# Three more warming matmuls at the start of a fused attention and MLP kernel, tied to the first chunk's statistics

## The chip, the cores and the metric

The kernel runs on one core of a Trainium2 chip. The metric is the device time of one execution in microseconds (us). The profiled span, from the first to the last instruction, is about 1.8 us shorter than the time (697.2 us against 695.4 in the profiled run of before).

## The reference, cut to what matters

```python
xn = layernorm(x)                      # x: 2048 tokens x 1024
out = x + attention(xn, wq, wk, wv, wo, beta) + mlp(layernorm(xn), w1, b1, w2, b2)
# mlp mixes tokens: u = gelu(h^T @ w1 + b1)   (contracts over the 2048 tokens)
```

The first product that TensorE can do is `h^T @ w1`, where h is the normalized input. It contracts over tokens, so it can begin as soon as the first chunk of 128 tokens is normalized, and it continues chunk by chunk (16 chunks).

## The kernel before: the parts that matter

The kernel has a small helper that follows every buffer as a resource with a last writer and a list of readers. A new operation waits for the last writer of what it reads, and for the last writer and all readers of what it writes:

```python
for r in reads:
    add(r.w)
    ...
for r in writes:
    ...
    for t in r.r.values():     # every recorded reader since the last write
        add(t)
```

At the start, while the input is being loaded, TensorE multiplies a zeroed tile ten times. Nobody reads the result:

```python
with fw.group(reads=[self.R_warm], writes=[self.R_bank[0]]):
    for _ in range(self.N_WARM):           # N_WARM = 10
        fw.mm(self.bank(0), self.warm[:, 0:P], self.warm[:], start=True, stop=True)
```

The norm of the chunks is written as a string of words, which gives the order of the operations on each engine:

```python
NORM_ORDER = (["D0 A1 S0 d2 h0 A1' A3 S1 d2' h1"] + ...)
# D0: statistics of chunk 0 on VectorE (two bn_stats, one bn_aggr); d2, d2': the two halves for chunk 2
# A1, A1': statistics of chunk 1 on ScalarE (odd chunks are done there)
# S0: rstd(0): a tensor_scalar on VectorE, then a power on GpSimd
# h0: scale_h(0): h = (x - mean) * rstd, on VectorE; TensorE's first real matmul waits for it

def rstd(self, c):
    ...
    fw.op("dve", lambda e: e.tensor_scalar(var, ..., E_H, op0=ALU.mult, op1=ALU.add), reads=[R], writes=[R])
    #                                       R is self.R_st[c], the statistics of chunk c
    fw.op("pool", lambda e: e.tensor_tensor(rs, var, self.expo[:, 0:1], op=ALU.pow), reads=[R, ...], ...)
```

`rstd` **writes** `R_st[c]`: it adds the epsilon to the variance in place.

The softmax here doesn't subtract the row's maximum and nothing guards it: scores larger than these inputs give would overflow.

## Time and profile before

| | before |
|---|---|
| time, median of the first 3 runs | 697.68 us (697.3, 697.68, 699.26) |
| span of the profiled run | 695.4 us |
| TensorE busy | 685.7 us, 99% |
| warming matmuls | 1.25 to 5.70 us, starts 0.427 us apart |
| granted clock turns full (record in the trace) | 5.84 us |
| first real matmul | 7.09 us, the next ones 0.216 us apart |

The granted clock is the profile's record of TensorE's clock, as a share of its full one. In this trace, equal matmuls start 0.427 us apart before it turns full at 5.84 us and 0.216 us apart after. Warming matmuls are there to be busy early, so that it turns full before real work; what that is worth is measured in run 7, where with four of them the real matmuls are 0.427 us apart until 10.5 us.

The page's busy times. Each entry is an engine's busy time, its share of the span and its number of instructions.

```profile
## 1 busy us (share of the span) xinstructions
PE 685.7 (99%) x4746; PEld 326.5 (47%) x4830; DVE 257.2 (37%) x581; ACT 277.7 (40%) x333; POOL 100.4 (14%) x156
```

The waits of TensorE (PE) over the whole span: who was waited for, us in total, how many times, the longest.

```profile
PE ps_all L194 <- DVE h L656: 1.4, 1, 1.4
PE ps_all L194 <- DVE brow L517: 1.3, 1, 1.3
PE ps_all L194 <- issue: 0.3, 2, 0.2
```

PE never waits for another engine for long after its first real matmul. So the kernel is bound by PE from then on, and whatever moves that first matmul moves the end.

The timeline of the start. Columns: start in us, duration in us, engine, line, operation, output and inputs with their shapes; in brackets how long the engine had been idle before, and who ended that. VectorE is DVE and GpSimd is POOL.

```profile
1.25 4.45 PE L194 MATMUL ps_all<-warm 128*128 128x512 bf16 x10 [1.25 <-DVE brow L517]
5.05 0.21 DVE L620 BATCH_NORM_AGGREGATE ln_mv<-ln_st 128x2 f32<-128x12 f32 x1
5.29 0.15 DVE L639 TENSOR_SCALAR ln_mv<-ln_mv 128x1 f32<-128x1 f32 x1
5.53 0.55 POOL L641 TENSOR_TENSOR ln_rs<-ln_mv,expo 128x1 f32<-128x1 f32 x1 [3.96 <-DVE ln_mv L639]
5.94 0.69 DVE L617 BATCH_NORM_STATS2 ln_st<-xin 128x6 f32<-128x512 bf16 x1 [0.49 <-DMA xin<-in_A_x_dram]
6.55 0.72 DVE L656 TENSOR_SCALAR h<-xin,ln_mv,ln_rs 128x512 bf16<-128x512 bf16 x2
7.09 1.46 PE L194 MATMUL ps_all<-h,w1early 128*128 128x512 bf16 x6 [1.39 <-DVE h L656]
```

This is the chain S0 (L639), power (L641), d2 (L617, which waited for the load of chunk 2), h0 (L656), first real matmul. PE is idle for 1.39 us between warming and work. DVE takes its instructions in order. Here h0 stands behind d2 and starts at 6.55 us, as d2 is ending.

### The profile page before, as it was taken

Reading aid. Unit: us, or ns where it says so; the run is one execution under the profiler, and the core shown is the slowest. Engines: PE = TensorE matmul, PEld = TensorE weight load, DVE = VectorE, ACT = ScalarE, POOL = GpSimd, SP = SyncE. Lnnn points to the kernel's source line nnn. Section 1 sums busy time; section 2 is a strip of 40 time slices with the busy share of each in tenths; the row PEclk is TensorE's granted clock in tenths of the full one; section 3 lists DMA queues with packets and bytes.
Section 4 is the critical chain, followed back from the end, with each engine's and each line's share of the span. In section 5 each row is a group of like instructions: output and inputs, shape, how many; then the busy total and the mean of one; then the engine's idle time right before and its main releaser. Section 6 shows DMA issues by size and latency. Waiting matters only on the chain.

```text
span 695.4 us, 11228 instructions
## 1 busy us (share of the span) xinstructions
PE 685.7 (99%) x4746; PEld 326.5 (47%) x4830; DVE 257.2 (37%) x581; ACT 277.7 (40%) x333; POOL 100.4 (14%) x156
## 2 busy tenths in 40 slices
PE   8999999999999999999999999999999999999998
PEld 3444444444444444444444445444444444445454
DVE  7740000000011334333436455536445553434445
ACT  7521211111134444444455444454544444534440
POOL 2600000000001111111121211112121111121130
PEclk9999999999999999999999999999999999999999
DMA  9497684227036536645263544525273544437014
GB/s 315 110 218 175 151 224 123 77 60 140 1 133 121 109 67 131 115 109 126 47 129 95 117 95 90 129 47 137 64 150 80 97 95 73 97 64 152 9 31 137
DMA packets 210537, 77.17 MB, mean 111 GB/s; under 512 B 173112, under 2 KB 202808, under 8 KB 210488
## 3 DMA queue, kind: packets, MB, share of 16 engines
q1 hardware_dynamic: 210344, 76.42, 47.8%
q8 instruction: 38, 0.62, 0.4%
q14 instruction: 11, 0.09, 0.1%
q10 hardware_dynamic: 144, 0.03, 0.0%
HBM read 59.79 MB, written 5.24 MB: 94 GB/s over the span
## 4 chain that ended last, share of the span: by engine, by line
PE 97%; DMA 1%; issue 1%; SPq 1%; DVE 0%
PE ps_all L194 97%; DMA xin<-in_A_x_dram 1%; SPq L216 1%; DVE ln_st L617 0%; DVE fin L1051 0%; PE ps_all L200 0%
## 5 line engine op out<-in xcount | busy, mean ns | idle before, releaser
L194 PE MATMUL ps_all<-gT,w2h 128*128 128x512 bf16 x868 | 207.8, 380 | 1.6 <-issue 0.2
L811 ACT ACTIVATE pT<-ps_all 128x512 bf16<-128x512 f32 (+1 forms) x128 | 151.4, 1234 | 76.7 <-PE ps_all L194 76.7
L194 PE MATMUL ps_all<-h,w1s 128*128 128x512 bf16 x752 | 165.1, 379 | 0.8
L806 POOL TENSOR_SCALAR_AFFINE_SELECT pT<-pT 128x512 bf16<-128x512 bf16 x128 | 83.9, 680 | 557.5 <-ACT pT L811 557.5
L194 PEld LDWEIGHTS ps_all<-gT,w2h 128*128 128x128 bf16 x896 | 83.1, 98 | 105.7 <-issue 13.8
L194 PEld LDWEIGHTS ps_all<-h,w1s 128*128 128x128 bf16 x768 | 75.1, 98 | 90.6
L845 DVE CAST ost<-ps_all 128x264 bf16<-128x264 f32 (+1 forms) x128 | 49.2, 398 | 169.4 <-PE ps_all L194 169.3
L713 ACT ACTIVATE gT<-ps_all,b1c 128x512 bf16<-128x512 f32 x56 | 35.1, 687 | 142.0 <-PE ps_all L194 136.4
L755 DVE CAST kT<-ps_all 128x512 bf16<-128x512 f32 x32 | 22.0, 688 | 176.9 <-PE ps_all L194 176.9
L194 PE MATMUL ps_all<-xnT,wk 128*128 128x512 bf16 x256 | 60.5, 379 | 0.0
L194 PE MATMUL ps_all<-xnT,wq 128*128 128x512 bf16 x256 | 60.4, 378 | 0.0
L194 PEld LDWEIGHTS ps_all<-vA,pT 128*128 128x128 bf16 x1280 | 47.7, 96 | 22.6
L194 PE MATMUL ps_all<-wv_sb,xnT 128*128 128x512 bf16 x227 | 54.0, 379 | 1.6
L739 ACT ACTIVATE qT<-ps_all 128x512 bf16<-128x512 f32 x32 | 19.1, 597 | 77.8 <-PE ps_all L194 77.8
L194 PE MATMUL ps_all<-vA,pT 128*128 128x33 bf16 x1280 | 48.6, 178 | 0.0
L951 DVE SCALAR_TENSOR_TENSOR stg<-ps_all,b2c,stg 128x512 bf16<-128x512 f32 x32 | 24.0, 750 | 61.7 <-PE ps_all L194 61.6
L758 ACT ACTIVATE etmp<-kT 128x512 bf16<-128x512 bf16 x24 | 15.1, 629 | 59.0 <-DVE kT L755 59.0
L194 PEld LDWEIGHTS ps_all<-xnT,wk 128*128 128x128 bf16 x256 | 23.8, 98 | 23.1
L194 PEld LDWEIGHTS ps_all<-wv_sb,xnT 128*128 128x128 bf16 x256 | 23.5, 97 | 23.7
L194 PEld LDWEIGHTS ps_all<-xnT,wq 128*128 128x128 bf16 x256 | 23.4, 97 | 23.2
L773 ACT ACTIVATE vA<-ps_all 128x512 bf16<-128x512 f32 x32 | 19.2, 600 | 37.1 <-PE ps_all L194 37.1
L194 PE MATMUL ps_all<-qT,kT 32*128 32x384 bf16 (+3 forms) x512 | 31.9, 299 | 0.0
(70 smaller groups left out, 419.7 us busy)
## 6 DMA issues: line engine op xcount, KB each, us to landing
w2h<-in_B_w_dram SPq DMA_DIRECT2D x32, 448.0 KB, 4.8
w1s<-in_B_w_dram SPq DMA_DIRECT2D x12, 1024.0 KB, 5.8
wq<-in_A_wq_dram SPq DMA_DIRECT2D x32, 256.0 KB, 4.4
wk<-in_A_wk_dram SPq DMA_DIRECT2D x32, 256.0 KB, 5.1
stg<-in_A_x_dram SPq DMA_DIRECT2D x16, 256.0 KB, 3.0
out_dram<-stg SPq DMA_DIRECT2D x16, 256.0 KB, 2.0
xin<-in_A_x_dram SPq DMA_DIRECT2D x2, 1024.0 KB, 10.5
wv_sb<-in_A_wv_dram SPq DMA_DIRECT2D x2, 1024.0 KB, 9.0
```

The costliest lines, as they stand in the source:

```text
L194: ins = self.nc.tensor.matmul(*args, **kwargs)
L216: ins = es.eng.dma_start(out_ap, in_ap, transpose=True) if transpose else es.eng.dma_start(out_ap, in_ap)
L713: fw.op("act", lambda e: e.activation(self.gT[:, fc, half * 512:(half + 1) * 512], self.bank(b), ACT.Gelu_apprx_tanh, bias=self.b1c[:, fc: ...
L739: fw.op("act", lambda e: e.activation(self.qT[k][:], self.bank(b), ACT.Copy), reads=[self.R_bank[b]], writes=[self.R_qT[k]])
L755: fw.op("dve", lambda e: e.tensor_copy(self.kT[k][:], self.bank(b)), reads=[self.R_bank[b]], writes=[self.R_kT[k]])
L758: fw.op("act", lambda e: e.activation(self.etmp[1][:], self.kT[k][:], ACT.Exp), reads=[self.R_kT[k]], writes=[self.R_etmp[1]])
L773: fw.op("act", lambda e: e.activation(self.vA[i][:, c, :, 0:D_HEAD], self.bank(b).rearrange("p (h d) -> p h d", d=D_HEAD), ACT.Copy), read ...
L806: fw.op("pool", lambda e: e.affine_select(d, d, pattern=[[0, 4], [1, P]], compare_op=ALU.is_ge, fill=0.0, base=0, channel_multiplier=-1), ...
L811: self.fw.op("act", lambda e: e.activation(dst, src, ACT.Exp, scale=SCALE), reads=R_src, writes=R_dst)
L845: fw.op("dve", lambda e: e.tensor_copy(dst, self.ps[:, b, 0:n * VW]), reads=[self.R_bank[b]], writes=[self.R_ost[o][qb]])
L951: fw.op("dve", lambda e: e.scalar_tensor_tensor(dst, self.bank(b), self.b2c[:, c:c + 1], dst, op0=ALU.add, op1=ALU.add), reads=[self.R_ban ...
```

## The change

Its intent is to keep TensorE active in that gap, so that its clock is full when real work begins. Three more warming matmuls are issued, and they are made to wait for the first chunk's statistics so that they come late enough.

```diff
-        with fw.group(reads=[self.R_warm], writes=[self.R_bank[0]]):
-            for _ in range(self.N_WARM):
+        self.keep_warm(self.N_WARM)
+
+    def keep_warm(self, n, reads=()):
+        fw = self.fw
+        with fw.group(reads=[self.R_warm, *reads], writes=[self.R_bank[0]]):
+            for _ in range(n):
                 fw.mm(self.bank(0), self.warm[:, 0:P], self.warm[:], start=True, stop=True)
...
-    NORM_ORDER = (["D0 A1 S0 d2 h0 A1' A3 S1 d2' h1"] +
+    NORM_ORDER = (["D0 W0 A1 S0 d2 h0 A1' A3 S1 d2' h1"] +
...
+            elif kind == "W":
+                self.keep_warm(3, [self.R_st[c]])
```

## The prediction

The forecast's sum came to 698.4 us: the times of before, plus the delay of the first real matmul (0.65 to 1.4 us), less what unlucky runs win back. Without that term, the two lower times of before (697.3 and 697.68) plus the 0.9 us as in the profile give 698.2 to 698.6 us. An unlucky phase is a start in which the clock turns full only after real work has begun; that there are such starts was a guess when this was written, and run 1 shows one.

> **What bounds the kernel now.** TensorE. The page gives PE 685.7 of 695.4 us (99%), and the chain of waits is 97% matmuls. PE's waits are only at the start: 1.3 us for the first memset, then 1.4 us before the first real matmul (`h,w1early`). So what moves the first real matmul (7.09 us) moves the end alike. From that one on they start every 0.216 us: the clock is full.
>
> **The start of before, from the timeline.** Ten warming matmuls start at 1.25 us, 0.427 us apart (slow clock); the last ends at 5.70. The trace's record of the granted clock turns full at 5.84 us. PE is idle from 5.70 to 7.09. DVE meanwhile: statistics of chunk 0 end at 5.26, the small tensor_scalar on its variance (L639) 5.29 to 5.44, POOL's power 5.53 to 6.08, statistics of chunk 2 from 5.94 (waited for its load), first half of h0 from 6.55, PE at 7.09.
>
> [...] full clock 4.6 us after PE's start. In an unlucky phase, before would get it only after real work began[...]. The times 697.3, 697.68 and 699.26 would fit two lucky runs and an unlucky one: a guess.
>
> **What the change does.** Its three matmuls wait for chunk 0's aggregation (5.26 us), which is earlier than the tenth warming matmul lets go (5.49), so that wait is free. They fill 5.49 to about 6.5 us (clock granted as in the profile) or to 6.98 us (all slow: 2 × 0.427 + 0.634 after 5.49).
>
> **The hidden cost.** The new group is recorded as a reader of chunk 0's statistics, R_st[0]. The next writer of that resource is the L639 tensor_scalar of chunk 0. It must now wait until the warming matmuls are done, which protects nothing. DVE is in order, so chunk 2's statistics, h0, S1 and h1 all move too. From the same steps of chunk 1 in the trace, tensor_scalar start to h start is 0.91 us; h0 start to PE's first matmul is 0.54 us. So PE starts at T + 1.45, T being the end of the warming plus about 0.05: about 8.0 us (+0.9) as in the profile, 8.5 us (+1.4) if all slow, 7.75 (+0.65) in the luckiest phase. The gap is moved rather than filled. After that DVE needs 1.33 us a chunk and PE 1.73: nothing more is lost or regained.
>
> **Gain.** The warming activity lasts to 6.5–7.0 us, so more phases get full clock before real work[...]. Fewer outliers, slower fast runs.
>
> **Prediction:** 698.4 us, 8 in 10 between 697.5 and 699.4. Faster by over 2%: 0.005; within 2%: 0.99; slower: 0.005.
>
> **What would show it.** Right: 13 warming matmuls; DVE's first L639 at about 6.6–7.1 us, waiting for PE, instead of 5.29; first real matmul at 7.75–8.5 us; all later work shifted equally; a smaller spread of times. Wrong: L639 still at 5.3 us and PE at 7.1; or PE stalling later, so that the delay is absorbed.
>
> **What would make it wrong.** [...]

## The result, and the profile after

The ratios are the mean time of one kernel's fast runs over that of the other's of the same rounds, so they are not quite the ratio of the medians.

| | before | after |
|---|---|---|
| median of 6 runs each | 697.53 us (697.14 to 699.26) | 697.95 us (697.7 to 698.36) |
| ratio | | 1.0001, 95% interval 0.9988 to 1.0014 |
| span of the profiled run | 695.4 us | 696.5 us |
| first real matmul | 7.09 us | 8.20 us |
| from the first real matmul's start to the last matmul's start | 685.798 us | 685.794 us |

The last line is worked out from the start times in the two traces. All work after the start takes the same time to 4 ns, so the start alone explains the difference of the two profiled runs: 1.11 us later at the first real matmul, 1.1 us more at the end.

The same lines of the timeline, after (S0 is now L645, the power L647, d2 L623, h0 L662):

```profile
1.25 5.38 PE L194 MATMUL ps_all<-warm 128*128 128x512 bf16 x13 [1.25 <-DVE brow L517]
4.93 0.21 DVE L626 BATCH_NORM_AGGREGATE ln_mv<-ln_st 128x2 f32<-128x12 f32 x1
6.74 0.15 DVE L645 TENSOR_SCALAR ln_mv<-ln_mv 128x1 f32<-128x1 f32 x1 [1.60 <-PE ps_all L194]
6.81 0.68 DVE L623 BATCH_NORM_STATS2 ln_st<-xin 128x6 f32<-128x512 bf16 x1
6.98 0.55 POOL L647 TENSOR_TENSOR ln_rs<-ln_mv,expo 128x1 f32<-128x1 f32 x1 [5.41 <-DVE ln_mv L645]
7.64 0.73 DVE L662 TENSOR_SCALAR h<-xin,ln_mv,ln_rs 128x512 bf16<-128x512 bf16 x2
8.20 0.38 PE L194 MATMUL ps_all<-h,w1early 128*128 128x512 bf16 x1 [1.57 <-DVE h L662]
```

The third line is the important one. S0, a 0.15 us operation on one value per row, had its input ready at about 5.1 us and stood idle for 1.60 us, released by PE. PE's warming ended at 6.63 us. The waits of DVE in the first 10 us show this wait as new, and the wait of 0.49 us for chunk 2's load gone, since d2 now comes after a later S0. Before, there were two waits for loads, chunk 0's (2.3 us) and chunk 2's:

```profile
DVE ln_st L617 <- DMA xin<-in_A_x_dram: 2.8, 2, 2.3
```

After, only chunk 0's is left, and S0's wait for PE has come:

```profile
DVE ln_st L623 <- DMA xin<-in_A_x_dram: 2.2, 1, 2.2
DVE ln_mv L645 <- PE ps_all L194: 1.6, 1, 1.6
```

The gap before the first real matmul is 1.57 us, where it had been 1.39. The added matmuls did not fill it; they pushed it.

Why, then, is the ratio 1.0001 and not 1.0016? The times of before are not all alike, and the experiments had to say how.

### The profile page after: what moved, and what is told of

Same layout as the page of the kernel before. It is cut to its first block, busy times and chain, and to the rows that moved or that the text cites. A ratio compares the mean times of both kernels' runs of the same rounds, so it can differ in the third digit from the quotient of the medians.

```text
span 696.5 us, 11235 instructions
## 1 busy us (share of the span) xinstructions
PE 686.7 (99%) x4749; PEld 326.8 (47%) x4833; DVE 257.2 (37%) x581; ACT 277.6 (40%) x333; POOL 100.1 (14%) x156
## 4 chain that ended last, share of the span: by engine, by line
PE 99%; issue 1%; DVE 0%; POOL 0%; DVEq 0%
PE ps_all L194 99%; POOL ln_rs L647 0%; DVE h L662 0%; DVE fin L1057 0%; DVE warm L515 0%; PE ps_all L200 0%; DVE ln_mv L645 0%; DVE brow L517 0%; DVEq L69 0%
```

## The experiments

The main theory has two parts. (1) The three matmuls are recorded as readers of `R_st[0]`, and S0 writes it, so S0 waits for them (a write-after-read wait), and everything behind it on DVE waits too. (2) What the change gains is in executions in which the clock turned full only after real work had begun. The rivals: the three matmuls delay the work simply by occupying PE or by waiting for the statistics; and the spread of before is noise that has nothing to do with the start.

The runs came in three calls. Kernels of one call share a chip and the runs of the kernel before, and each call was on another chip.

### 1. Before, unchanged

> The kernel before, unchanged, as a null control and for another look at the clock. Theory (two kinds of execution: the clock is granted either before or after the first real matmul at about 7.1 us): times fall in two groups, about 697.2 and about 698.5 to 699.3, and the profile shows the granted clock either before 7.1 us with every real matmul 0.216 us apart, or later, with the first real matmuls 0.427 us apart. Rival (the spread is noise from elsewhere): the start looks the same in every profile whatever the time. Ratio to before 1.000 within 0.001.

Measured: 698.2 us median of 6 runs, ratio 1.0004 (0.9991 to 1.0017). This profile was taken on an execution of the slower kind, 698.52 us, span 696.8. The stretch from 7.10 to 9.80 us of both executions of the same kernel, first the one of the beginning (columns: stretch, its length, busy time and number of matmuls in it, granted clock, DMA share, GB/s):

```profile
7.10:9.80 2.70, 2.70 (x13) 1.00 1.04 379
```

and this one:

```profile
7.10:9.80 2.70, 2.70 (x7) 1.00 1.01 358
```

PE is fully busy in both, but does 13 matmuls in one and 7 in the other. Here the real matmuls start 0.427 us apart, and 0.216 us apart only from about 10 us on. From the first real to the last matmul this execution took 687.27 us, 1.47 us more than the other. Its start is otherwise the same (first real matmul at 6.95 us). Beware of the column of the granted clock: it says 1.00 in both. In this trace there is no record of the clock's change at all, and where there is one, the stretches before it are shown as 1.00 too (5.00 to 5.80 us in the first profile, with the record at 5.84). The spacing of equal matmuls is the better witness.

All 41 runs of before fall into two groups with nothing between 697.88 and 698.52: 24 runs with a mean of 697.33 us, and 17 with a mean of 698.81. The difference, 1.48 us, is the 1.47 us of the trace. So the two starts differ as the theory says, which the rival of noise from elsewhere does not explain. That all 17 are slow-clock starts is inferred from this match and from one trace of each kind; if so, they are not rare: 17 of 41.

### 2. After, unchanged

> The changed kernel, unchanged, in the same rounds as the variants. Theory (write-after-read wait moves the start of the work by 0.65 to 1.4 us, and the clock is always granted in time): times 697.7 to 698.4, no run below 697.6 and none above 698.8; L645 waits about 1.5 us for PE; first real matmul at 7.75 to 8.5 us. Rival (the three matmuls are free and the difference is noise): times from 697.2 on.

Measured: 697.8 to 698.62 us, ratio 1.0008 (0.9996 to 1.002). S0 at 6.29 us after waiting 1.0 us for PE; first real matmul at 7.746 us. In this execution the clock turned full at 4.70 us by its record, so the warming ended sooner, at 6.17 us; the prediction had given 7.75 us for this case. That it fits so exactly is partly luck: the warming ended 0.08 us earlier than the 6.25 us behind that figure, and the way from there to the work was 0.08 us longer. The wait for PE was shorter than the "about 1.5 us" that I wrote, for that reason. Over both calls, after has 11 runs, from 697.7 to 698.62, with a mean of 698.13. It has one group only, between the two of before: 0.81 us above its fast group, 0.68 us below its slow one. No trace shows an execution of after with a slow-clock start.

### 3. The same matmuls without the dependence

```diff
-    N_WARM = 10
+    N_WARM = 13
```

(on the kernel before)

> Thirteen warming matmuls in one group, none of which reads the statistics: the same PE work as the change, without its dependence. Theory (the write-after-read wait is the cost): the small tensor_scalar of chunk 0 is back at about 5.3 us, the first real matmul at about 7.1 us, clock granted by about 7 us; times 697.1 to 697.6 in nearly every run, about 0.7 to 0.9 us below the changed kernel, and a smaller spread than before. Rival (three more matmuls occupy PE and that is the delay): first real matmul at about 8 us and times as the changed kernel, about 698.

Measured: 697.89 us median, five runs 696.86, 696.98, 697.89, 697.89, 697.91; ratio 0.9996 (0.9984 to 1.0008). None of the five lies in my range of 697.1 to 697.6. S0 was back at 5.17 us, as the theory says, though PE did all 13 matmuls. But the first real matmul was at 7.81 us, which no theory had expected. The timeline says why:

```profile
5.17 0.15 DVE L639 TENSOR_SCALAR ln_mv<-ln_mv 128x1 f32<-128x1 f32 x1
5.41 0.55 POOL L641 TENSOR_TENSOR ln_rs<-ln_mv,expo 128x1 f32<-128x1 f32 x1 [3.84 <-DVE ln_mv L639]
6.66 0.69 DVE L617 BATCH_NORM_STATS2 ln_st<-xin 128x6 f32<-128x512 bf16 x1 [1.33 <-DMA xin<-in_A_x_dram]
7.27 0.72 DVE L656 TENSOR_SCALAR h<-xin,ln_mv,ln_rs 128x512 bf16<-128x512 bf16 x2
7.81 0.81 PE L194 MATMUL ps_all<-h,w1early 128*128 128x512 bf16 x3 [1.01 <-DVE h L656]
```

The power for chunk 0 was done at 5.96 us, but h0 stands behind d2 on DVE, and d2 waited until 6.66 us for the load of chunk 2, which had come at 5.94 us in the first profile of before. It may be a second, smaller source of spread: the two groups of this kernel's times, 0.9 us apart, would fit it, but only one of the five was traced. The run doesn't decide against occupancy by its time, only by S0. The next three do.

### 4. The same change, one word moved

```diff
-    NORM_ORDER = (["D0 W0 A1 S0 d2 h0 A1' A3 S1 d2' h1"] +
+    NORM_ORDER = (["D0 A1 S0 W0 d2 h0 A1' A3 S1 d2' h1"] +
```

The three matmuls still wait for the statistics, in fact for S0 itself. But S0 is the last writer of `R_st[0]`, so nobody waits for them.

> The change with its word W0 moved behind S0: the three matmuls still wait for the first chunk's statistics (now for the tensor_scalar at about 5.4 us), but no writer of that resource comes after them. Theory (write-after-read): as the thirteen without a wait, first real matmul at about 7.1 us, 697.1 to 697.6. Rival (waiting for the statistics itself, or PE occupancy, is the cost): as the changed kernel, about 698, first real matmul at about 8 us.

Measured: 697.1 us median (696.93 to 697.67), ratio 0.9993 (0.9981 to 1.0005).

```profile
1.25 5.22 PE L194 MATMUL ps_all<-warm 128*128 128x512 bf16 x13 [1.25 <-DVE brow L517]
5.17 0.15 DVE L645 TENSOR_SCALAR ln_mv<-ln_mv 128x1 f32<-128x1 f32 x1
5.85 0.69 DVE L623 BATCH_NORM_STATS2 ln_st<-xin 128x6 f32<-128x512 bf16 x1 [0.52 <-DMA xin<-in_A_x_dram]
6.46 0.72 DVE L662 TENSOR_SCALAR h<-xin,ln_mv,ln_rs 128x512 bf16<-128x512 bf16 x2
7.00 1.67 PE L194 MATMUL ps_all<-h,w1early 128*128 128x512 bf16 x7 [0.53 <-DVE h L662]
```

Thirteen warming matmuls, a wait for the statistics, and the first real matmul at 7.00 us. The gap is now 0.53 us. Neither occupancy nor the wait on the statistics is the cost.

The same kernel was run once more later on:

> The change with W0 behind S0 once more, for more samples in the same rounds. Theory: no run above 698.1; median 697.1 to 697.5, about 0.8 us below the changed kernel's eleven runs so far (mean 698.15) and below the mean of before by about 0.6.

Measured: 697.13 us median (696.76 to 697.44), ratio 0.9989 (0.9977 to 1.0002), first real matmul at 6.86 us. (The mean of the changed kernel's eleven runs is 698.13, not the 698.15 of this expectation.)

### 5. The wait kept in its place, the record of the reader taken away

```diff
-        with fw.group(reads=[self.R_warm, *reads], writes=[self.R_bank[0]]):
+        with fw.group(reads=[self.R_warm], writes=[self.R_bank[0]], extra=[r.w for r in reads]):
```

The matmuls use none of the statistics, so nothing can race.

> The change with its order kept, but the three matmuls wait for the aggregation's token without being recorded as readers of the statistics (they use none of that data, so nothing races). Theory (write-after-read): the small tensor_scalar of chunk 0 back at about 5.3 us, first real matmul at about 7.1 us, times 697.1 to 697.6. Rival (the wait of PE for the statistics costs): as the changed kernel, about 698.

Measured: 697.26 us median (697.17 to 697.71), ratio 0.999 (0.9977 to 1.0003). S0 at 5.12 us, first real matmul at 7.27 us (d2 waited for its load until 6.11 us here):

```profile
5.12 0.15 DVE L645 TENSOR_SCALAR ln_mv<-ln_mv 128x1 f32<-128x1 f32 x1
6.11 0.69 DVE L623 BATCH_NORM_STATS2 ln_st<-xin 128x6 f32<-128x512 bf16 x1 [0.84 <-DMA xin<-in_A_x_dram]
7.27 2.10 PE L194 MATMUL ps_all<-h,w1early 128*128 128x512 bf16 x9 [0.91 <-DVE h L662]
```

The write-after-read part of the theory holds with the order of the words untouched.

### 6. One and six recorded readers

```diff
-                self.keep_warm(3, [self.R_st[c]])
+                self.keep_warm(1, [self.R_st[c]])      # and 6 in the other kernel
```

> One recorded reader instead of three. Theory (write-after-read, DVE waits for the end of the last recorded warming matmul): it ends at about 6.1 us, the small tensor_scalar starts at about 6.15, the first real matmul at about 7.6 us, 0.5 us later than before and 0.5 us earlier than with three. Rival (occupancy of PE): about 7.1 us, since PE is free by 6.1.

> Six recorded readers instead of three. Theory (write-after-read): the warming ends about 0.65 us later than with three if the clock is full by then (3 x 0.216), up to 1.28 us later if slow; the small tensor_scalar and the first real matmul move by the same amount, to 8.7 to 9.5 us; times 698.4 to 699.5. Rival (occupancy): PE is free at about 7.2 to 8.2 us, so the first real matmul would be at no more than about 8.2.

Measured for one: 697.84 us median of 4 (697.4 to 699.04), ratio 1.0 (0.9984 to 1.0017); S0 at 6.25 us, first real matmul at 7.70. Measured for six: 698.4 us median of 4 (698.33 to 698.83), ratio 1.0007 (0.9992 to 1.0022); S0 at 6.78, first real matmul at 8.24. The position for six missed my range of 8.7 to 9.5 us, because I had started from the run whose clock turned full at about 6.1 us (by the spacing of its matmuls), and in this one it was at 4.78. What the write-after-read theory says without knowing the clock is that the first real matmul follows the end of the warming at a fixed distance. It does:

| kernel (profiled run) | end of the warming | first real matmul | difference |
|---|---|---|---|
| three readers, first profile | 6.628 us | 8.200 us | 1.572 |
| three readers, second profile | 6.167 | 7.746 | 1.579 |
| one reader | 6.129 | 7.701 | 1.572 |
| six readers | 6.657 | 8.235 | 1.578 |
| ten matmuls, three of them readers (run 8) | 6.090 | 7.663 | 1.573 |
| nothing for S0 to wait for: before, twice | 5.701, 5.700 | 7.090, 6.946 | 1.389, 1.246 |
| nothing for S0 to wait for: runs 3, 4 (twice), 5 | 6.807, 6.475, 6.264, 6.361 | 7.814, 7.000, 6.857, 7.269 | 1.007, 0.525, 0.593, 0.908 |

The ends of the warming are the profile's, which models the ends of matmuls; that S0 starts 0.11 to 0.12 us after that end in all five runs with readers is as much as these traces say of it.

### 7. Four warming matmuls

```diff
-    N_WARM = 10
+    N_WARM = 4
```

(on the kernel before)

> The kernel before with four warming matmuls instead of ten, so that warming ends at about 3.2 us. Theory (too little early activity leaves the clock slow when real work starts): the first real matmul is still at about 7.1 us, but the matmuls after it are 0.427 us apart for a few us until the clock is granted [...]; times 1.5 to 3 us above the fast runs of before, 698.7 to 700.2. If times stay at 697.2, the warming matmuls have no worth and the spread of before has another cause.

Measured: 698.94 us median of 4 (698.84 to 700.55), ratio 1.0021 (1.0001 to 1.0041); the run at 700.55 lies above my range of 698.7 to 700.2. The first real matmul was at 6.72 us, earlier than in the two profiles of before, since chunk 2's load was early (d2 started at 5.33 us, right behind S0). But the matmuls were 0.427 us apart until 10.5 us, and the clock's record turns full at 10.87. From the first to the last real matmul it took 687.83 us, 2.03 us more than with a full clock. So warming has a worth, and part (2) of the theory holds from this side too.

### 8. The dependence without more work

```diff
-    N_WARM = 10
+    N_WARM = 7
```

(on the changed kernel: ten warming matmuls as before, the last three of them recorded readers)

> The dependence without extra work: ten warming matmuls as before, but the last three are the recorded readers of the statistics. Theory (write-after-read): they start at about 5.15 us, when the statistics are there, end at about 6.2 to 6.7, and the first real matmul is at the end of the warming plus 1.57 us as in the four runs with a reader so far, 7.8 to 8.3 us, though PE does no more work than before. Rival (the number of matmuls is the cost): first real matmul at about 7.1 us.

Measured: the first real matmul at 7.66 us, S0 at 6.21 after waiting 0.99 us for PE, 1.573 us from the end of the warming to the work:

```profile
1.25 3.17 PE L194 MATMUL ps_all<-warm 128*128 128x512 bf16 x7 [1.25 <-DVE brow L517]
5.27 0.82 PE L194 MATMUL ps_all<-warm 128*128 128x512 bf16 x3 [0.85 <-DVE ln_mv L626]
6.21 0.15 DVE L645 TENSOR_SCALAR ln_mv<-ln_mv 128x1 f32<-128x1 f32 x1 [0.99 <-PE ps_all L194]
7.66 0.81 PE L194 MATMUL ps_all<-h,w1early 128*128 128x512 bf16 x3 [1.57 <-DVE h L662]
```

The first real matmul is a little below my range of 7.8 to 8.3, since the clock turned full at 5.16 us and the three ran fast. The matmul count is that of before, and the delay is there: it is the dependence. The times are 697.76, 700.22, 700.28 and 700.68 us, ratio 1.0027 (1.0008 to 1.0046). The profile fell on the first of these. I had given no time for it. The three at 700 would fit a late start with a late clock on top, and the warming is interrupted here from 4.42 to 5.27 us. But no trace shows one of them, and no run shows what such a gap does to the clock, so this stays open.

### 9. h0 ahead of d2

```diff
-    NORM_ORDER = (["D0 W0 A1 S0 d2 h0 A1' A3 S1 d2' h1"] +
+    NORM_ORDER = (["D0 A1 S0 W0 h0 d2 A1' A3 S1 d2' h1"] +
```

> The change with W0 behind S0, and h0 moved ahead of d2 as well. In the runs so far, h0 stands behind d2 on DVE, and d2 waits for the load of chunk 2, which landed between 5.3 and 6.7 us; in the thirteen without a wait it landed at 6.66 us and the first real matmul was at 7.81. Theory (the second spread of the times, 696.9 against 697.9, is this landing): with h0 first, the first real matmul is at about 6.7 us in any case, bounded by the statistics of chunk 0, and no run is above 697.7. Since h1 then comes a little later, PE may wait for it at chunk 1, so the fastest runs could be up to 0.2 us slower than with d2 first. Rival (the second spread is not from this landing): same two groups of times, 696.9 and 697.9.

Measured: 697.19 us median (697.14 to 697.52), ratio 0.9992 (0.9978 to 1.0006). First real matmul at 6.71 us, as expected. But PE then waited in the first 12 us:

```profile
PE ps_all L194 <- DVE brow L517: 1.3, 1, 1.3
PE ps_all L194 <- DVE ln_mv L645: 0.6, 1, 0.6
PE ps_all L194 <- DMA w1early<-in_B_w_dram: 0.4, 1, 0.4
PE ps_all L194 <- DVE h L662: 0.2, 1, 0.2
```

The third line is the wait before the first real matmul:

```profile
6.71 1.89 PE L194 MATMUL ps_all<-h,w1early 128*128 128x512 bf16 x8 [0.43 <-DMA w1early<-in_B_w_dram]
```

The profile puts it down to a load of weights, but the matmul starts 0.56 us after h0 (6.15 us), as in the other runs (0.54 to 0.56), so that load held it up by next to nothing. The last line, 0.2 us for h, is new and lies inside the work. It is at chunk 1: from 8.21 to 8.79 us two matmuls start 0.58 us apart instead of 0.216. The work as a whole took 0.39 us longer (686.18 us from the first to the last real matmul), 0.36 of it there. So the earlier start (0.29 us against run 4) was given back at chunk 1. The spread of the five runs is 0.4 us, the smallest here, and there is no second group; the median is that of run 4. That agrees with the landing of chunk 2 as the second source of spread, but five runs are few for it.

## Why the prediction was right, and where it was off

The time, 697.95 us, lay in the range of 697.5 to 699.4 around 698.4, and the sum was made of the right terms. The time alone is a weak test, since the median of before, 697.53, lies in that range too; the starts in the trace are the stronger one.

- **What bounds it.** Right. From the first real matmul on, the work takes 685.79 to 685.92 us in 10 of the 13 profiles. The other three are the two with a slow clock in the work and the one with h0 first.
- **The hidden wait.** Right in kind and place. S0 waited for PE, 1.60 us, and it goes away with the reader's record (run 5), with the order (run 4), and comes without any additional matmul (run 8). Its reach was a little undersized: from the end of the warming to the first real matmul I took 1.50 us, and it measured 1.57. With warming that ended at 6.63 us instead of 6.5, this is why the first real matmul came at 8.20 us and not at the forecast 8.0.
- **The wait on the statistics being free.** Right: the eleventh matmul started at 5.495 us, 0.427 after the tenth, as if there were no wait. (In run 2, where the clock turned full at 4.70 us, PE seems to have waited a little: the warming ended 0.88 us after the statistics, 6.17 against 5.29 us, as in run 8, 6.09 against 5.21, where the profile shows that wait.)
- **The gain in unlucky phases.** Right in kind: 1.47 to 1.48 us were measured. The share of such phases was a guess from three runs, one in three. It is 17 of 41. That is the term that moved the ratio: against the fast group the change costs 0.81 us, against the slow one it wins 0.68. The mean over all runs is 697.94 us before and 698.13 after, and the ratio of six runs each happened to be 1.0001, which is luck.
- **Not seen.** I took the arrival of chunk 2 at 5.94 us as fixed. It moved d2's start from 5.33 to 6.66 us among the runs, and h0 stands behind it.

Two kernels have lower means than both. With W0 behind S0, ten runs have a mean of 697.19 us; with the token alone, five have 697.34. All fifteen together are 697.24, which is 0.70 us (0.10%) below the mean of before. Each single ratio's interval still reaches 1, since before scatters so much. The firmer sign is in the groups: of the 25 runs of the kernels with thirteen warming matmuls for which S0 does not wait (runs 3, 4, 5 and 9), none lies above 697.91 us, where before, with ten, has 17 of 41 above 698.5, and with four (run 7) all 4 are.

## What to carry to other kernels

An operation that only needs to come after something should wait for it without being recorded as a reader; otherwise the next writer of that resource waits in turn, and on an engine that takes its instructions in order, as DVE does here (after the change S0 started 1.45 us later, and h0 behind it 1.09), so does all that is behind it. Ask of each new dependence not only what it waits for but who will now wait for it. When the runs of a kernel form two groups, look at the first few microseconds of one of each before judging a change by its mean: here the loss in one group and the gain in the other cancelled to a ratio of 1.0001, and in ten runs moving one word kept the gain without the loss.

## What the traces show of the clock, and what they do not

- How much PE must do for its clock to turn full, and over what stretch, was not shown. PE's first matmul starts at 1.25 us in each of these. By the trace's record the clock then turned full at 3.89 us with h0 first, 4.70 in run 2, 4.78 with six readers, 5.16 in run 8 and 5.84 in the first profile of before; by the spacing of the matmuls, at about 6.1 us in the first profile of after. In the slow run of before, whose warming ended at 5.70 us as in the fast one, the matmuls were 0.427 us apart until about 10 us. With four warming matmuls, ending at 3.14 us, the record turns full at 10.87 us. These are single executions.
- A slow start cost 1.47 us of 697, 0.2%, by the two traces of before. But 17 of its 41 runs lie in a second group that far away (1.48 us), which is more than the change that was to be judged (0.81 us against the fast group).
- The trace's events of the clock can be missing altogether. Four of 13 profiles here had no record of the change to a full clock, one of them of an execution whose matmuls were 0.427 us apart until about 10 us.
